# Moving two loads to ScalarE's queue and shortening the store runs of two late chunks in a TensorE-bound pointwise convolution

## Chip, cores, metric

One core of one Trainium2 chip. The metric is device time in microseconds (us); small differences are read from the profile of one execution, since whole runs of one kernel differ by 0.3% and more. Engines: PE = TensorE, DVE = VectorE, ACT = ScalarE, SP = SyncE.

## The reference

A depthwise separable convolution with a 1x1 depthwise kernel: scale each channel by `dw`, then multiply by `pw`.

```python
# x (1,384,384,384), dw (1,1,384), pw (384,384), all bfloat16
out = xp * dw[0, 0]
return jnp.einsum('bhwc,cd->bhwd', out, pw)
```

147,456 rows of 384 channels: 113 MB in, 113 MB out.

## The kernel before

At the start it folds `dw` into `pw` on TensorE (the "weight stage": 18 matmuls, copied to `w_r`). Then 288 "supertiles" of 512 rows pass through: VectorE transposes blocks of x into T, TensorE runs 48 matmuls into one of two PSUM halves, ScalarE copies that half to O, SyncE stores O. x arrives in chunks of 1 to 10 supertiles; SyncE issues all loads and stores but one.

```python
LMAX = 10; NR = 3; LONG = 3
head, tail = [[1, 1, 2, 2, 4]], [[6, 4], [3, 2, 1, 1, 1]]   # supertiles per chunk
...
        def load_x(t):
            ...
            if first + LONG < NS:
                src = rows.rearrange("(p s) c -> p (s c)", p=P)                # long packets
            else:
                src = rows.rearrange("(a k q) c -> q a k c", k=4, q=4)         # 768-byte packets
            if i == 0 and g >= NR:
                nc.sync.wait_ge(s_t[je % 2][1], je // 2 + 1)                   # buffer free
            nc.sync.dma_start(dst, src).then_inc(s_x[g % NR][i], 16)

        def store(t):
            if first + LONG < NS:
                dst = rows.rearrange("(q p j) d -> p q (j d)", q=4, p=P)       # runs of j x 768 bytes
            else:
                dst = rows.rearrange("(m q) d -> m (q d)", q=4)                # 3072-byte runs
            nc.sync.wait_ge(s_a[je % 2], je // 2 + 2)
            if je + 1 == NS:
                nc.sync.wait_ge(s_d, 1)                                        # VectorE's half of the last copy
            nc.sync.dma_start(dst, src).then_inc(s_o[g % NR], 16)

        nc.scalar.dma_start(dw_row[:], ...)
        nc.sync.dma_start(pw_n[:], ...)
        # ... then all loads and stores on SyncE, in the order in which they become possible
```

For a chunk of one supertile either the load or the store is cut into 768-byte packets (the traces hold 1536 loaded packets of that size between 511 and 553 us in the kernel before; the last store shows as 128 packets of 3072 bytes). `LONG = 3` gives the last three chunks long stores and short-packet loads.

## Time and profile before

| | before |
|---|---|
| time, 3 runs | 575.43 us (575.23 to 576.05) |
| span of the profile | 573.7 us |
| main stretch of TensorE starts | 7.18 us |
| 288 supertiles x 1.95 us | 561.6 us |
| last output copies start | 569.0 us |
| last store issued, landed | 570.06, 572.37 us |

Read it as head + TensorE + tail (the head: up to the start of the main stretch; the tail: from the start of the last output copies to the end of the span, 4.7 us here). TensorE never pauses in the main stretch, so only the first 7 and the last 5 us are open to a change in transfers, unless a transfer makes TensorE pause. The profile's lines are with the prediction below.

### The profile page before, as it was taken

Reading aid. Unit: us, or ns where it says so; the run is one execution under the profiler, and the core shown is the slowest. Engines: PE = TensorE matmul, PEld = TensorE weight load, DVE = VectorE, ACT = ScalarE, POOL = GpSimd, SP = SyncE. Lnnn points to the kernel's source line nnn. Section 1 sums busy time; section 2 is a strip of 40 time slices with the busy share of each in tenths; the row PEclk is TensorE's granted clock in tenths of the full one; section 3 lists DMA queues with packets and bytes.
Section 4 is the critical chain, followed back from the end, with each engine's and each line's share of the span. In section 5 each row is a group of like instructions: output and inputs, shape, how many; then the busy total and the mean of one; then the engine's idle time right before and its main releaser. Section 6 shows DMA issues by size and latency. Waiting matters only on the chain.

```text
span 573.7 us, 29706 instructions
## 1 busy us (share of the span) xinstructions
PE 567.3 (99%) x13869; PEld 414.9 (72%) x13869; DVE 509.3 (89%) x583; ACT 418.8 (73%) x296; POOL 0.9 (0%) x8
## 2 busy tenths in 40 slices
PE   8999999999999999999999999999999999999996
PEld 5777777777777777777777777777777777777774
DVE  6899999999999999999999999999999999999994
ACT  6777777777777777777777777777777777777775
POOL 0000000000000000000000000000000000000000
PEclk9999999999999999999999999999999999999999
DMA  8999999999999999999999999999999999994996
GB/s 324 432 409 417 430 397 430 444 424 422 399 408 416 384 397 436 398 383 395 432 398 384 395 429 390 393 401 429 402 385 419 401 390 397 425 394 149 402 408 251
DMA packets 25912, 226.88 MB, mean 395 GB/s; under 512 B 1197, under 2 KB 5678, under 8 KB 22062
## 3 DMA queue, kind: packets, MB, share of 16 engines
q1 hardware_dynamic: 25900, 226.79, 98.0%
q14 instruction: 9, 0.07, 0.0%
q8 instruction: 1, 0.02, 0.0%
q10 hardware_dynamic: 2, 0.00, 0.0%
HBM read 113.54 MB, written 113.25 MB: 395 GB/s over the span
## 4 chain that ended last, share of the span: by engine, by line
PE 98%; DMA 1%; ACT 0%; DVE 0%; issue 0%; SPq 0%
PE ps L166 97%; DMA pw_n<-in_pw_dram 1%; PE ps L216 1%; DMA out_dram<-O 0%; ACT O L307 0%; DVE O L304 0%; SPq L337 0%; SPq L100 0%
## 5 line engine op out<-in xcount | busy, mean ns | idle before, releaser
L166 PE MATMUL ps<-w_r,T 32*128 32x384 bf16 x13824 | 561.8, 321 | 0.1
L258 DVE STREAM_TRANSPOSE T<-X 128x384 uint32<-128x384 uint32 x576 | 506.2, 882 | 54.0 <-DMA X<-in_x_dram 2.4
L307 ACT CAST O<-ps 128x1536 bf16<-128x1536 f32 x288 | 413.5, 1436 | 147.9 <-PE ps L166 147.9
L166 PEld LDWEIGHTS ps<-w_r,T 32*128 32x128 bf16 x13824 | 412.9, 93 | 149.2 <-issue 0.7
L271 ACT CAST w_r<-ps 128x768 bf16<-128x768 f32 x5 | 3.7, 805 | 1.7 <-PE ps L216 1.6
L183 PE MATMUL ps<-zero 32*128 32x384 bf16 x24 | 2.6, 494 | 1.4 <-POOL zero L232 1.4
L304 DVE CAST O<-ps 128x768 bf16<-128x768 f32 x1 | 1.0, 958 | 3.0 <-DMA out_dram<-O 3.0
L216 PE MATMUL ps<-pw_n,sel_w 64*128 64x384 bf16 x18 | 3.0, 510 | 0.1
L183 PEld LDWEIGHTS ps<-zero 32*128 32x128 bf16 x24 | 0.7, 100 | 2.6 <-issue 2.6
L216 PEld LDWEIGHTS ps<-pw_n,sel_w 64*128 64x128 bf16 x18 | 1.2, 138 | 1.6 <-issue 1.2
L244 ACT ACT_TABLE_LOAD x1 | 1.3, 1283 | 1.5 <-SPq L100 1.5
L276 DVE TENSOR_REDUCE sel<-eye 128x64 f32<-128x128 bf16 x1 | 0.3, 290 | 1.8 <-POOL eye L234 1.8
L271 DVE CAST w_r<-ps 128x768 bf16<-128x768 f32 x1 | 1.0, 956 | 1.0 <-PE ps L216 1.0
L286 DVE TENSOR_SCALAR sel_w<-sel,dw_f 128x256 bf16<-128x256 f32 x3 | 0.9, 348 | 0.0
L283 DVE COPY dw_f<-ps 128x3 f32<-128x3 f32 x1 | 0.2, 161 | 0.8 <-PE ps L198 0.8
L198 PEld LDWEIGHTS ps<-ones,dw_row 1*128 1x128 bf16 x3 | 0.2, 98 | 0.2 <-issue 0.2
L244 ACT COPY warm<-warm 128x1 f32<-128x1 f32 x2 | 0.3, 188 | 0.0
L234 POOL TENSOR_SCALAR_AFFINE_SELECT eye<-ones 128x128 bf16<-128x128 bf16 x1 | 0.3, 292 | 0.1
L232 POOL MEMSET zero<- 128x192 uint32 x1 | 0.3, 258 | 0.0
L198 PE MATMUL ps<-ones,dw_row 1*128 1x1 bf16 x3 | 0.2, 159 | 0.0
L233 POOL MEMSET ones<- 128x128 bf16 x1 | 0.2, 204 | 0.0
L231 POOL MEMSET warm<- 128x3 f32 x1 | 0.1, 101 | 0.5 <-SPq L100 0.5
(4 smaller groups left out, 0.4 us busy)
## 6 DMA issues: line engine op xcount, KB each, us to landing
X<-in_x_dram SPq DMA_DIRECT2D x26, 3840.0 KB, 21.5
out_dram<-O SPq DMA_DIRECT2D x26, 3840.0 KB, 27.5
X<-in_x_dram SPq DMA_DIRECT2D x2, 1536.0 KB, 17.4
out_dram<-O SPq DMA_DIRECT2D x2, 1536.0 KB, 13.7
X<-in_x_dram SPq DMA_DIRECT2D x3, 768.0 KB, 8.8
out_dram<-O SPq DMA_DIRECT2D x3, 768.0 KB, 8.9
X<-in_x_dram SPq DMA_DIRECT2D x1, 2304.0 KB, 18.9
out_dram<-O SPq DMA_DIRECT2D x1, 2304.0 KB, 12.1
```

The costliest lines, as they stand in the source:

```text
L166: mm = nc.tensor.matmul(PS[s][:, q, :D], lhsT=Ts[s][32 * q : 32 * q + 32, b, par::2], rhs=w_r[32 * q : 32 * q + 32, b, par, :], start=(b, ...
L183: nc.tensor.matmul(PS[0][:, i, :D], lhsT=zero[32 * i : 32 * i + 32, 0:P], rhs=zero[32 * i : 32 * i + 32, :], start=True, stop=True, tile_p ...
L198: mm = nc.tensor.matmul(PS[1][:, 0, D + k : D + k + 1], lhsT=dw_row[:, P * k : P * k + P], rhs=ones[0:1, 0:1], start=True, stop=True,)
L216: mm = nc.tensor.matmul(PS[(k + 1) % 2][:, 2 * r + v, :D], lhsT=sel_w[64 * v : 64 * v + 64, k, r, :, :].rearrange("p q w -> p (q w)"), rhs ...
L232: nc.gpsimd.memset(zero[:].bitcast(U32), 0).then_inc(s_zero)
L234: nc.gpsimd.affine_select(out=eye[:], in_=ones[:], pattern=[[-1, P]], compare_op=mybir.AluOpType.is_equal, fill=0.0, base=0, channel_multi ...
L244: c = nc.scalar.copy(warm[:, s + 1 : s + 2], warm[:, 0:1])
L258: ins = nc.vector.transpose(out=Tw[:, 3 * h : 3 * h + 3], in_=Xw[:, :, j, 96 * h : 96 * h + 96].rearrange("p k (b w) -> p b k w", w=32),)
L271: o = nc.vector.tensor_copy(out, in_) if e == 0 else nc.scalar.copy(out, in_)
L286: nc.vector.tensor_scalar_mul(sel_w[:, k], sel[:].unsqueeze(2).to_broadcast([P, 2, 4, 32]), dw_f[:, k : k + 1]).then_inc(s_sw)
L304: e = nc.vector.tensor_copy(Ov[:, nq:4, j, :], PS[s][:, nq:4, :D])
L307: a = nc.scalar.copy(Ov[:, 0:nq, j, :], PS[s][:, 0:nq, :D])
```

## The change

Its intent: one load of the slow 768-byte kind (109 GB/s between 528.5 and 530 us in the profile of before, where the transfers around have some 400) in place of three, that one away from SyncE's queue; and the first x chunk issued beside `pw` instead of behind it.

```diff
-LONG = 3
+LONG = 1
-        def load_x(t):
+        def load_x(t, eng=nc.sync):
...
-            if i == 0 and g >= NR:
+            if g >= NR and (i == 0 or eng is not nc.sync):
...
-            nc.sync.dma_start(dst, src).then_inc(s_x[g % NR][i], 16)
+            eng.dma_start(dst, src).then_inc(s_x[g % NR][i], 16)
...
         nc.scalar.dma_start(dw_row[:], ...)
+        load_x(0, nc.scalar)
         nc.sync.dma_start(pw_n[:], ...)
...
-            todo.append((g_end[g - NR] if g >= NR else -1, load_x, t))
+            if 0 < t < NT - LONG:
+                todo.append((g_end[g - NR] if g >= NR else -1, load_x, t))
...
             a.then_inc(s_a[s])
+            if jj == g_end[len(groups) - 1 - NR] + 1:      # supertile 260
+                for u in range(NT - LONG, NT):
+                    load_x(u, nc.scalar)
```

More of the change, by code (lines that the diff above doesn't have):

```diff
@@ L109, in load_x @@
                 src = rows.rearrange("(a k q) c -> q a k c", k=4, q=4)
-            if i == 0 and g >= NR:
+            if g >= NR and (i == 0 or eng is not nc.sync):
                 je = g_end[g - NR]
-                nc.sync.wait_ge(s_t[je % 2][1], je // 2 + 1)
-            nc.sync.dma_start(dst, src).then_inc(s_x[g % NR][i], 16)
+                eng.wait_ge(s_t[je % 2][1], je // 2 + 1)
+            eng.dma_start(dst, src).then_inc(s_x[g % NR][i], 16)
         def store(t):
```

## The prediction

Head +0.45, middle 0, tail +0.05, together +0.5 us on 575.43, so 575.9 us. But the head's +0.45 rests on an assumption, that the packets of the two queues alternate one for one, which no trace had shown when it was made; the counts per engine in it are estimates, packets counted in the trace over the profile's 16 engines. Rival (a)'s 520 to 527 us is an estimate too, from SyncE's three long issues (513.05 to about 530.8 us) and the assumption that ScalarE's would be caught behind them.

> **What bounds the kernel now.** I read the page first (busy shares, then the chain that ended last), then the chain in order of time, then the timeline of the first 10 us, of the stretch around 510 to 530 us, and of the last 5 us, and then the DMA view of short windows. The page and the chain in order of time:
>
> ```profile
> PE 567.3 (99%) x13869; PEld 414.9 (72%) x13869; DVE 509.3 (89%) x583; ACT 418.8 (73%) x296; POOL 0.9 (0%) x8
> PEclk9999999999999999999999999999999999999999
> ...
> 1.01 3.03 DMA pw_n<-in_pw_dram
> 4.05 0.05 issue
> 4.09 2.96 PE ps L216 x18
> 7.05 0.12 issue
> 7.18 557.91 PE ps L166 x13728
> 565.08 0.02 issue
> 565.11 1.45 ACT O L307
> 566.55 0.02 issue
> 566.57 2.46 DMA out_dram<-O
> 569.02 0.94 DVE O L304
> ```
>
> PE is busy 99% at full clock, and the chain is one unbroken PE stretch from 7.18 us on. The starts of ScalarE's output copies confirm it: they stand 1.95 us apart to the end, one per supertile of 48 matmuls, and 288 x 1.95 = 561.6 us is what those matmuls take. (The chain's last two pieces, a store and then the VectorE copy, are an attribution slip: that copy at 569.01 waits for PE's last matmul, as ScalarE's copy at 569.00 does; the semaphore it waits for besides was long satisfied.) So the span of 573.7 us is 7.18 us of head, 561.6 us of PE, and about 4.9 us of tail. A change in transfers can move the time only in three ways: by moving the landing of pw_n (the chain's first piece), by making PE wait in the middle, or by moving the landing of the last store.
>
> The head, from the timeline:
>
> ```profile
> 0.97 0.49 ACTq L131 DMA_DIRECT2D dw_row<-in_dw_dram  x1
> 1.01 0.45 SPq L132 DMA_DIRECT2D pw_n<-in_pw_dram  x1
> 1.49 1.28 ACT L244 ACT_TABLE_LOAD   x1 [1.49 <-SPq L100]
> 1.52 3.49 SPq L113 DMA_DIRECT2D X<-in_x_dram  x7
> 4.09 0.13 PEld L216 LDWEIGHTS ps<-pw_n,sel_w 64*128 64x128 bf16 x4 [0.47 <-DMA pw_n<-in_pw_dram]
> 4.63 3.80 ACT L271 CAST w_r<-ps 128x768 bf16<-128x768 f32 x5 [1.56 <-PE ps L216]
> 5.83 1.55 DVE L258 STREAM_TRANSPOSE T<-X 128x384 uint32<-128x384 uint32 x2
> 8.00 1.57 DVE L258 STREAM_TRANSPOSE T<-X 128x384 uint32<-128x384 uint32 x2 [0.62 <-DMA X<-in_x_dram]
> ```
>
> PE waits for pw_n at 4.09. It does not wait for x: the first transposes (5.83) start without idle time before them, right behind VectorE's weight copy, so the first chunk of x, which landed at 5.0 us, was there in time. VectorE waits 0.62 us for the second chunk, but PE does not notice: the copies from 9.36 us on are already 1.95 us apart. ScalarE has 1.56 us idle before its first weight copy.
>
> The middle, where the three loads of 768-byte packets are issued, in the timeline of SyncE's queue:
>
> ```profile
> 511.42 1.59 SPq L113 DMA_DIRECT2D X<-in_x_dram  x3
> 513.05 8.79 SPq L113 DMA_DIRECT2D X<-in_x_dram  x1
> 521.89 4.44 SPq L113 DMA_DIRECT2D X<-in_x_dram  x1
> 526.38 4.41 SPq L128 DMA_DIRECT2D out_dram<-O  x1
> ```
>
> The reader should see that an issue is normally 0.35 to 0.5 us, but here three in a row hold the queue for 8.79, 4.44 and 4.41 us. In the window 528.5 to 530 us the DMA share is only 0.34 of 16 engines and the rate 109 GB/s, with nearly all packets under 2 KB[...]. It costs nothing: the copies stay 1.95 us apart, since this data is first used near 553 us.
>
> [...]the issues of dw_row (0.97 to 1.46) and pw_n (1.01 to 1.46) overlap almost wholly, neither longer than its neighbours of 0.43 to 0.50 us.[...]
>
> **The change part by part.**
>
> Head: the first x load leaves SyncE's queue, where it was third in line behind pw_n, and goes to ScalarE's, right behind dw_row. Issue time there about 1.5 to 2.0 us, the same as before (1.52).[...] pw_n is 384 packets of 768 bytes, 24 per engine; in the window 2 to 3 us, 229 such packets took 67.5% of 16 engine-us, so 47 ns each, about 1.1 us per engine. The x chunk is 128 packets of 3072 bytes, 8 per engine; in the window of the last store, 570.8 to 572.1 us, 128 such packets took 76.9% of 16 x 1.3 us, so 125 ns each and 1.0 us per engine. pw_n's packets begin about 2.1 us; those of x, half a microsecond later by issue, about 2.6. By 2.6 about a quarter to a third of pw_n has started. If packets alternate one for one, 8 x-packets of 125 ns fall among the remaining 17, and pw_n ends up to 1.0 us later; the engines are only about two thirds busy between 2 and 3 us, so a good half of that falls into time that was idle. I take +0.45 us, with 0 (x still behind[...]) to +0.9 as the bounds. All of it lies on the chain: 18 weight matmuls start at 4.5 instead of 4.09 and the main stretch at 7.6. Nothing is gained in return: x0 was not waited for by PE, and the other chunks going out 0.5 us earlier only shortens VectorE's unfelt waits. ScalarE's second issue pushes its table load to 2.0 and its end to about 3.3, plus 0.3 for two copies = 3.6, still ahead of 4.63.
>
> Middle: [...]SyncE's long blocks vanish. Worth 0, as there is some 40 us of slack. The third is issued by ScalarE after the copy that starts at 516.36 and ends at 517.80:
>
> ```profile
> 516.36 1.44 ACT L307 CAST O<-ps 128x1536 bf16<-128x1536 f32 x1 [0.51 <-PE ps L166]
> 518.30 1.44 ACT L307 CAST O<-ps 128x1536 bf16<-128x1536 f32 x1 [0.51 <-PE ps L166]
> ```
>
> ScalarE idles 0.51 us per supertile, and a copy may be another 0.51 us late (1.95 - 1.44) before PE lacks its PSUM half, so an issue up to about 1.0 us is free. The first such load on SyncE was the third of the group of 1.59 us, so at most about 0.75 us. Expected cost 0. Its wait for transposes of supertile 259 is over: they finished by 511.4, when SyncE's load with the same wait went out.
>
> Tail: the last store is unchanged, 3072-byte runs. The two before it now write 768-byte runs: 32 per engine; in the window 32 to 34 us, 855 packets, nearly all 768-byte, took 102.4% of 32 engine-us, 38 ns each, so 1.2 us against 1.0. The last store is issued at 570.06, its packets run from about 570.9, and the store before it was issued 1.5 us earlier. There is a gap between them of some 0.3 us, so +0.2 us mostly vanishes: I take +0.05.
>
> Sum: +0.45 + 0 + 0.05 = +0.5 us, 575.43 + 0.5 = 575.9 us.
>
> **The rivals.** (a) ScalarE's issue in the middle is caught behind SyncE's blocked one. At 516.4 SyncE now issues the 3840 KB store, with four loads and a previous store (issued 496.37, landed about 525) still queued. [...]ScalarE sits until perhaps 520 to 527 us; less the 1.0 us that is free, PE loses 2 to 8 us: 578 to 584 us. For it: [...]8.79 us of blocking seen on SyncE. Against it: dw_row and pw_n did not delay each other[...]. I give it one in four. (b) [...]pw_n is not disturbed at all: then the head costs 0 and the time is 575.4 to 575.5. (c) Earlier x helps the start: it would need PE to have waited for x; the chain and the 1.95 us spacing say it did not. At most 0.1 us gain. (d) The two 768-byte stores delay the last store by their full 0.2 us each: 576.2.
>
> **Range and chances.** The main case lies between 575.2 and 576.4; rival (a) stretches the upper side. I take 575.1 to 579.5. Faster by 2% would need 11.5 us off a PE stretch that nothing touches: 0.01. Slower by 2% needs a ScalarE stall of over 12 us: 0.03.
>
> **What would show it.** In the chain of the changed kernel, the piece of pw_n should end near 4.5 instead of 4.05 and the L166 stretch begin near 7.6; if it begins at 7.18, the alternation step is wrong. ScalarE's issue near 517.8 should last under 1 us and the copies stay 1.95 us apart; a longer issue and a gap in the PE stretch is rival (a). SyncE's issues at 511 to 513 should all be under 1 us. The last store should land about 3.4 us after PE's end, as now; more would mean the tail step is wrong. The whole is wrong if PE's pace itself changes.

## The result and the profile after

576.14 us median (576.01 to 576.58, 6 runs), against 575.47 us (575.14 to 576.05, 6 runs) for the kernel before in the same rounds. Ratio 1.0011, 95% interval 0.9999 to 1.0024. Ratios here are the mean time of one kernel's fast runs over that of the other's of the same rounds, so not quite the ratio of the medians quoted.

The profile's span grew from 573.70 to 574.27 us, and where it grew is not where the prediction put it. The chain of the changed kernel, in order of time (start, length, what):

```profile
4.49 2.21 ACT w_r L273 x3
6.71 0.14 issue
6.84 561.80 PE ps L168 x13824
...
568.67 0.96 DVE O L306
```

The main stretch starts at 6.84 us, 0.34 earlier, and is as long as before. It no longer waits for the weight matmuls but for ScalarE's three copies of their results. The head, from the timeline:

```profile
1.54 0.37 ACTq L113 DMA_DIRECT2D X<-in_x_dram  x1
3.95 0.13 PEld L218 LDWEIGHTS ps<-pw_n,sel_w 64*128 64x128 bf16 x4 [0.33 <-DMA pw_n<-in_pw_dram]
```

`pw_n` landed at 3.88 us, not later than before (4.05). That gives less than half of the 0.34 us, 0.14 (its first matmul starts at 3.95 instead of 4.09). The rest is the weight stage. Its matmuls' group on the page of before, then of after (busy us, mean ns of one):

```profile
L216 PE MATMUL ps<-pw_n,sel_w 64*128 64x384 bf16 x18 | 3.0, 510 | 0.1
```
```profile
L218 PE MATMUL ps<-pw_n,sel_w 64*128 64x384 bf16 x18 | 2.2, 380 | 0.0
```

Those of them that ran between 5.3 and 6.2 us took 524 ns each before and 325 ns after. In the trace of before, those that start up to 6.31 us took 496 to 524 ns each, and the last two (6.62 us) 424 and 421; in the changed kernel those up to 4.25 us took 496 to 524, two at 4.57 us 451 and 447, and the rest, from 4.86 us on, 319 to 333. The first record of granted clock in the two traces, 1.00, begins at 6.82 and at 4.82 us; before it they hold no record. So the faster pace came 2.0 us earlier in the changed kernel's profile. What sets that moment is not shown. Over all 14 profiles the mean of this group lay between 380 and 521 ns, and it was 502 ns when only the head was changed (`head_only` below): the moved chunk does not fix it, and luck of the run is the natural reading. It is not proved: the nine profiles with the first chunk on ScalarE's queue have 380 to 502 ns (median 414), the five with it on SyncE's 445 to 521 (median 482), and no run tests whether the move shifts the moment.

The middle went as hoped. From the timeline of SyncE's and of ScalarE's queue around 511 us:

```profile
511.08 1.84 SPq L113 DMA_DIRECT2D X<-in_x_dram  x4
516.02 1.44 ACT L309 CAST O<-ps 128x1536 bf16<-128x1536 f32 x1 [0.51 <-PE ps L168]
516.03 0.65 ACTq L113 DMA_DIRECT2D X<-in_x_dram  x1
```

SyncE's long blocks are gone. ScalarE's issue lasts 0.65 us, and it starts with the copy rather than after it: the queue issues while the engine copies, and the next copy starts at 517.97 us, 1.95 us after this one, so it costs nothing at all.

The tail is what grew. The last issue in the timeline of SyncE's queue, the instructions' line in the DMA view of the last 3 us (packets, MB, share of 16 engines), and the store's own line there (KB, us from issue to landing):

```profile
570.08 0.34 SPq L128 DMA_DIRECT2D out_dram<-O  x1
...
q14 instruction: 1, 0.01, 0.6%
...
out_dram<-O SPq DMA_DIRECT2D x1, 384.0 KB, 2.8
```

VectorE's part of the last copy ends at 568.67 + 0.96 = 569.63 us, yet the store goes out at 570.08: 0.45 us of idle queue, where before it was 0.09 (569.97 to 570.06). Then the store takes 2.85 us to land, where it took 2.31. Sum: -0.34 (head) + 0.36 (idle) + 0.54 (landing) = +0.56 us, against 574.27 - 573.70 = 0.57. And in that window one packet of the queue that the profile calls "instruction" (q14, 8192 bytes, at 571.08 us) comes amid the last store's packets. Before, it came at 569.07, ahead of the last store. I call such a packet a fetch, and take it for one of instructions.

### The profile page after: what moved, and what is told of

It is laid out like the page before. It is cut to its first block, busy times and chain, and to the rows that moved or that the text cites. A ratio compares the mean times of both kernels' runs of the same rounds, so it can differ in the third digit from the quotient of the medians.

```text
span 574.3 us, 29706 instructions
## 1 busy us (share of the span) xinstructions
PE 566.5 (99%) x13869; PEld 414.7 (72%) x13869; DVE 507.3 (88%) x583; ACT 419.0 (73%) x296; POOL 0.9 (0%) x8
## 4 chain that ended last, share of the span: by engine, by line
PE 98%; ACT 0%; DVE 0%; issue 0%; POOL 0%; POOLq 0%; SPq 0%
PE ps L168 98%; PE ps L185 0%; ACT w_r L273 0%; DVE O L306 0%; PE ps L218 0%; POOL zero L234 0%; POOL warm L233 0%; PE ps L200 0%; POOLq L343 0%; SPq L100 0%
## 5 line engine op out<-in xcount | busy, mean ns | idle before, releaser
L168 PE MATMUL ps<-w_r,T 32*128 32x384 bf16 x13824 | 561.8, 321 | 0.7 <-ACT w_r L273 0.7
```

Source lines behind the costliest of these rows:

```text
L168: mm = nc.tensor.matmul(PS[s][:, q, :D], lhsT=Ts[s][32 * q : 32 * q + 32, b, par::2], rhs=w_r[32 * q : 32 * q + 32, b, par, :], start=(b, ...
```

## The experiments

The question: is the tail's loss due to the 768-byte stores (theory A1), or to the place of SyncE's instruction fetch, which moves because two issues left SyncE's code (A2)? And does the first chunk's new queue do anything? The runs came in three calls of four kernels each, each call on another chip, each with 5 rounds against the kernel before. All outputs were correct. "SyncE code" counts instructions against before. In the expectation of `head_only`, theory A stands for A1 and A2 together.

| kernel | SyncE code | times, us | ratio [95%] | main start | copy start to last issue | issue to landing | last fetch at |
|---|---|---|---|---|---|---|---|
| before | 0 | 575.23 to 576.05 | | 7.18 | 1.06 | 2.31 | 569.07 |
| changed | -2 | 576.01 to 576.58 | 1.0011 [0.9999, 1.0024] | 6.84 | 1.41 | 2.85 | 571.08 |
| `head_only` | -1 | 575.35 to 577.17 | 1.0000 [0.9984, 1.0016] | 7.09 | 1.07 | 2.88 | 570.87 |
| `long1_sync` | 0 | 575.35 to 576.52 | 0.9996 [0.9982, 1.0010] | 7.07 | 1.05 | 2.32 | 569.79 |
| `after_x0_sync` | -1 | 575.57 to 576.22 | 0.9996 [0.9981, 1.0011] | 7.23 | 1.06 | 2.58 | 570.85 |
| `after_again` | -2 | 575.69 to 576.22 | 1.0000 [0.9985, 1.0015] | 6.84 | 1.41 | 2.54 | 570.74 |
| `after_pad2` | -2+2 | 575.22 to 575.74 | 0.9999 [0.9986, 1.0012] | 6.98 | 1.06 | 2.31 | 569.10 |
| `after_pad8` | -2+8 | 575.07 to 576.15 | 0.9994 [0.9981, 1.0007] | 7.06 | 1.05 | 3.16 | 535 |
| `long3_rest` | -2 | 575.70 to 579.24 | 1.0025 [1.0007, 1.0043] | 6.99 | 1.44 | 3.99 | 572.31 |
| `before_again` | 0 | 575.27 to 577.88 | 1.0015 [0.9997, 1.0033] | 7.04 | 1.05 | 2.31 | 568.77 |
| `pad8_again` | -2+8 | 575.09 to 575.50 | 0.9997 [0.9983, 1.0010] | 7.17 | 1.06 | 2.32 | 535 |
| `pad8_long3` | -2+8 | 575.26 to 575.85 | 1.0001 [0.9987, 1.0014] | 6.95 | 1.06 | 2.83 | 539 |
| `pad8_long0` | -1+8 | 575.73 to 576.47 | 1.0011 [0.9997, 1.0025] | 7.07 | 1.06 | 3.44 | 554 |
| `pad8_x0_sync` | -1+8 | 575.27 to 575.65 | 1.0000 [0.9986, 1.0014] | 7.08 | 1.06 | 2.41 | 554 |

The right-hand columns are of the one profiled execution of each kernel. With eight added instructions the last fetch in the table is another one: the changed kernel has a fetch at 534.8 us too, and the one that moved lies at 520.3 us in `after_pad8` and 520.4 in `pad8_again`. `before_again`: the same program against itself came out at 1.0015. Of the changes only the 1.0025 of `long3_rest` has an interval that excludes 1, and only just. So the reasons rest on the profiles and on where runs of several kernels fall, not on a ratio.

### Taking the change apart

**head_only**: before, with the first x chunk on ScalarE's queue.

```diff
         nc.scalar.dma_start(dw_row[:], ...)
+        load_x(0, nc.scalar)
```

> Only the first chunk of x moves to ScalarE's queue, behind the tiny dw row; all else as before. Theory A (the two short stores and the third load at the end cost the added 0.6 us; the head's gain of 0.34 us in the one profile is luck[...], since the weight matmuls' mean fell from 510 to 380 ns there while pw_n landed only 0.17 us earlier): time equal to before within 0.2 us, tail from last matmul to end of span 4.7 us as before; the head 6.8 or 7.2 us depending on the weight matmuls' mean. Theory B[...]: pw_n lands after 4.3 us and the time is +0.3 us or more. Theory C (the head move truly gains): -0.3 us against before.

Measured: median 575.95 us. `pw_n` landed at 3.96 us: the delay that my prediction expected (theory B) does not exist. The main stretch began at 7.09 us with weight matmuls of 502 ns: the 0.34 us gain of the first profile (theory C) does not follow from this move. But the tail was 5.3 us, not 4.7, with all three last stores in the old 3072-byte form: the store landed 2.88 us after its issue and the fetch fell at 570.87. Theory A1 cannot explain that.

**long1_sync**: before, with only the constant changed.

```diff
-LONG = 3
+LONG = 1
```

> Only the constant goes from 3 to 1, all loads stay on SyncE's queue: the stores of the last chunk but one and but two write 768-byte runs. Theory A1 (the short runs of the store before the last cost the tail): tail from last matmul to the span's end about 5.6 us as in the changed kernel, against 4.7 before; time +0.7 us with the same head. Theory A2 (the tail's loss comes from where an instruction fetch falls, 571.08 us in the changed kernel's profile, amid the last store, 569.07 before): the fetch moves since SyncE's or ScalarE's code differs, and the tail follows it, 4.7 to 5.6 us, whatever the run length.

Measured: median 575.80 us. Tail 4.70 us, landing 2.32 us, fetch at 569.79: short runs in the stores before the last cost nothing, as A2 says. This profile shows something else. Its chain, in order of time:

```profile
7.07 19.76 PE ps L166 x480
26.83 0.41 issue
27.24 542.31 PE ps L166 x13344
```

TensorE paused after exactly 10 supertiles (480 matmuls). VectorE's timeline around it, of this kernel and then of the kernel before:

```profile
26.28 4.36 DVE L258 STREAM_TRANSPOSE T<-X 128x384 uint32<-128x384 uint32 x6 [2.42 <-DMA X<-in_x_dram]
```
```profile
25.26 5.45 DVE L258 STREAM_TRANSPOSE T<-X 128x384 uint32<-128x384 uint32 x7 [1.37 <-DMA X<-in_x_dram]
```

The sixth chunk of x landed at 26.18 us here and at 25.16 before, where TensorE did not notice. The main stretch lasts 562.5 us here against 561.8, so the late chunk cost 0.7 us. An estimate from these figures: a landing 0.7 us earlier (25.5 us, or 25.6 with the start at 7.18) would have cost nothing, so the kernel before stands about 0.4 us from a pause that my reading (the waits for x are "unfelt") took for safe.

**after_x0_sync**: the changed kernel, first chunk back on SyncE.

```diff
-        load_x(0, nc.scalar)
-            if 0 < t < NT - LONG:
+            if t < NT - LONG:
```

> The changed kernel, but the first chunk of x stays on SyncE's queue. Theory A1 (short runs): tail about 5.6 us, time +0.7 us against before if the head is 7.18 us, +0.3 us if it is 6.84. If the head's move were a true gain of 0.34 us (theory C), this must be 0.3 us slower than the changed kernel in the same rounds. If the tail goes back to 4.7 us, neither the runs nor the third load are to blame, but the place of SyncE's code.

Measured: median 575.73 us. One instruction fewer on SyncE than before: no idle time ahead of the last store (1.06), but the fetch at 570.85 and landing 2.58 us. Theory C expected this kernel to be 0.3 us slower than the changed one; the medians are 575.73 and, for `after_again` in the same rounds, 575.99. But its tail was 0.3 us shorter (5.0 against 5.3), which would hide a gain of 0.3 us at the head, and the main start was 7.23 against 6.84: this pair does not settle C. The pair without a late fetch (`pad8_again`, `pad8_x0_sync`) starts at 7.17 and 7.08, against C.

**after_again**: the changed kernel unaltered.

> The changed kernel once more, to see what of its first profile repeats: the time 0.5 to 0.8 us above before; the tail of 5.6 us and the idle 0.41 us of SyncE ahead of the last store, if they are of the kernel; the head at 6.84 us again only if it is not luck[...].

Measured: median 575.99 us, 0.44 above before's median of these rounds (575.55), though the means are equal, since before's 11 runs reach from 575.14 to 577.14. The idle 0.45 us ahead of the last store repeats to the hundredth, and again a fetch falls amid that store. The early main start (6.84) came back too, with weight matmuls of 414 ns; later profiles of the same head start at 6.95 to 7.17. This time the chain before the main stretch is another one, in order of time:

```profile
1.54 4.31 DMA X<-in_x_dram
...
5.87 0.87 DVE T L260
...
6.84 561.81 PE ps L168 x13824
```

TensorE waits here for the first chunk of x itself. On ScalarE's queue that chunk landed at 5.29 to 6.09 us in nine profiles, on SyncE's at 4.88 to 5.06 in five: the load that was to come sooner comes later. In four of the nine (`after_again`, `after_pad2`, `long3_rest`, `pad8_long0`) the main stretch hangs on it, in none of the five.

### Moving SyncE's code and nothing else

**after_pad2** and **after_pad8**: the changed kernel, with two or eight instructions on SyncE that do nothing but raise an unused semaphore, after its first store.

```diff
+            if f is store and t == 0:
+                for _ in range(2):                         # 8 in after_pad8
+                    nc.sync.nop(nofuse=True).then_inc(s_pad)
```

> The changed kernel with two do-nothing instructions (increments of an unused semaphore) on SyncE after its first store, so that SyncE has as many instructions as in the kernel before. Theory A2 (SyncE's own instruction fetch falls into the last store because two issues left its code): the last 8192-byte fetch moves ahead of the last store (before 570.1 us), the idle time of SyncE ahead of the last store falls from 0.45 to about 0.1 us, the last store lands 2.3 us after its issue instead of 2.5 to 2.9, and the tail is 4.7 us instead of 5.3 to 5.6. Theory A1 (the 768-byte stores): nothing changes, tail 5.3 us or more.

Measured: 575.34 us median. Two do-nothing instructions give back the whole tail: idle 0.10 us, landing 2.31 us, tail 4.70 us, fetch at 569.10. The DMA view of the same final window (570.45 to 573 us, the share of the DMA engines in tenths in 40 slices) of the changed kernel, with its instruction queue's line, and then of this one, which has no such line:

```profile
DMA  0000000779797999999899720101010000000000
...
q14 instruction: 1, 0.01, 0.8%
```
```profile
DMA  4101999989797979797400000000000000000000
```

In the changed kernel the last store's packets start three slices (some 0.2 us) later, as it was issued 0.22 us later (570.08 against 569.86), and after the bulk of them a thin trail (the digits 2 0 1 0 1 0 1) runs on: its packets of 3072 bytes start at 571.98, 572.10, 572.22 and 572.33 us, one after the other, 121 ns each. Here it ends at once, and the instruction packet is not in the window.

> As the former, with eight. Theory A2: the fetch moves earlier still (some ten us before the end), tail 4.7 us, and with the fuller start of x the time is the lowest of all, 575.1 to 575.4 us in nearly every run, 0.6 us under the changed kernel. Theory A1: tail 5.3 us or more, time as the changed kernel.

Measured: median 575.08 us, four of five runs at 575.07 to 575.63, and the profiled one 576.15. In that profile the fetch had moved to 54 us from the end (a fetch at 520.3 us is new, and none comes after that at 535), the idle time was gone, and still the store landed 3.16 us after its issue. The DMA rate in 40 slices, 569 to 573 us, of this profile and of its repeat `pad8_again`:

```profile
GB/s 31 15 31 192 338 338 323 338 323 338 323 323 338 323 315 177 31 115 330 422 392 422 392 330 422 422 392 300 31 31 31 31 31 0 31 31 31 0 0 0
```
```profile
GB/s 23 23 23 23 146 323 346 307 353 323 315 353 315 323 353 315 200 39 31 369 399 399 492 307 399 430 369 461 246 31 0 0 0 0 0 0 0 0 0 0
```

The trail of 31 GB/s is one packet of 3072 bytes per 0.1 us slice, where such a packet takes some 0.12 us (124 ns on average in the last store of the kernel before). My estimate from these two figures is that one engine still works when the others are done; the traces do not name the engine of a packet. Without the trail, in the repeat, the store landed 0.84 us sooner after its issue (2.32). So a late landing has two candidates: the fetch (in all five profiles where one falls amid the last store, the landing took 2.54 us or more; in the four where it came just ahead of the issue, 2.31 or 2.32), and an engine that lags by chance of the run (theory D). The fetch's packet took 0.31 us in the changed kernel, less than the 0.54 us that its landing grew, so the fetch alone need not be all of it.

**long3_rest**: the changed kernel's two moved loads, with the old constant's stores and loads.

```diff
-LONG = 1
+LONG = 3        # the last load alone on ScalarE
```

> The change without its constant: the first chunk of x and the last load go on ScalarE's queue, but the last three chunks keep 3072-byte stores (and 768-byte loads). Theory A2: the tail is that of the changed kernel, 5.3 to 5.6 us, with 0.45 us of idle SyncE ahead of the last store, since SyncE has the same number of instructions; time as the changed kernel. Theory A1: tail 4.7 us, 0.6 to 0.9 us faster than the changed kernel.

Measured: median 576.88 us (575.70 to 579.24), on the same chip and in the same rounds as the padded kernels' 575.34 and 575.08. The idle time is there again (0.48 us), with three long stores: it belongs to the number of SyncE's instructions, not to the runs. The last store landed only 3.99 us after its issue, with a fetch at 572.31 and a trail of 42 to 113 GB/s up to some 572.8 us. Theory A2 gets its idle time here, but not its number for the tail: 6.8 us, not 5.3 to 5.6, and the ratio of 1.0025 is worse than the changed kernel's two (1.0011, 1.0000; other chips).

**before_again**: no edit.

> The kernel before, once more, for a second profile of it. If the sixth chunk of x (the second group of ten) is on a knife's edge, landing 25 to 26 us and wanted by 25.8, then of its runs some are near 575.2 and others 0.7 us or more above, and the profile shows either a landing under 25.8 us and no gap in TensorE's stretch, or a later one and a gap; the tail is 4.7 us in either case. The main stretch starts at 6.8 to 7.2 us with the mean of the weight matmuls between 380 and 520 ns.

Measured: 575.27 to 577.88 us; four runs at 575.27 to 575.68, two at 577.85 and above. The profile fell on a fast one: sixth chunk at 24.81 us, no pause, tail 4.69 us. What the two long runs did is not in a profile.

### The parts, with the fetch out of the way

**pad8_again**: as `after_pad8`.

> The changed kernel with eight do-nothing SyncE instructions, again: in its first trial four of five runs were at 575.07 to 575.63 and the profiled one at 576.15, where one or two DMA engines were still busy with an earlier store when the last one came (landing 3.16 us after issue with no fetch near). Theory A2 plus D (D: an engine that lags at the end, by chance of the run, delays the last store): most runs 575.0 to 575.4, none above 576.6, no fetch after 560 us; tail 4.7 us or, where an engine lags, more. If instead A2 is wrong, its times are those of the changed kernel, 575.7 to 576.6.

Measured: 575.09 to 575.50, tail 4.70 us. Of all fifteen runs of the padded changed kernel, fourteen lie at 575.74 or below; of the eleven runs of the changed kernel, two do (575.69, 575.73). The chips differ, so this is no ratio; the kernel before had medians of 575.47 and 575.55 beside the changed kernel and of 575.44 and 575.34 beside the padded one.

**pad8_long3**: as `long3_rest`, with the eight instructions.

> The same with the last three chunks in the old form: 3072-byte stores, and three loads of 768-byte packets[...], two of them on SyncE. Theory D: [...]an engine that lags is likelier; then the times have a long upper tail (one or more of six above 576.6), a median 0.3 us or more above its sibling with the constant 1, and the last store lands more than 2.5 us after its issue in the profile if that run is a long one. If the constant does not matter, its times are those of its sibling.

Measured: 575.26 to 575.85, median 0.2 us above its sibling, none above 576.6. The upper tail that theory D expected is absent, in this kernel and in the kernel before of these rounds (575.19 to 575.88). A late landing shows in the profile (2.83 us without a fetch near), but that the three 768-byte loads make it likelier is not shown.

**pad8_long0**: no chunk in the old form, so the last store too in 768-byte runs. The last load then goes back to SyncE's queue, as the loop for ScalarE's late load is empty.

```diff
-LONG = 1
+LONG = 0
```

> The same with no chunk in the old form: [...]the last store too writes 768-byte runs, 32 packets of about 38 ns per engine instead of 8 of 125, so its landing should take 2.5 us instead of 2.3 us from its issue: +0.2 us against its sibling with 1. Theory D: no run above 576.6 us. If the run length mattered more than its packets[...], landing over 3 us.

Measured: median 576.42 us; 575.73 twice, 576.42 to 576.47 three times. The median is 1.2 us above its sibling's, and the runs do not overlap (575.09 to 575.50 there). In the profiled run the last store landed 3.44 us after its issue, where the sibling took 2.32. That is more than the packet count gives (+0.2 us, the estimate above), and the rate again trails off at the end, at 23 to 27 GB/s; with five runs the two cannot be separated. In this kernel the last store should stay in long runs.

**pad8_x0_sync**: first chunk on SyncE.

```diff
-        load_x(0, nc.scalar)
-            if 0 < t < NT - LONG:
+            if t < NT - LONG:
```

> The same as the changed kernel with eight do-nothing instructions, but the first chunk of x on SyncE's queue. Theory E (the second queue fills the DMA engines early, so that the sixth chunk of x lands near 23.9 us instead of 24.6 to 26.2): 4 to 6 us moves 250 to 320 GB/s instead of 390 to 425, the sixth chunk lands 24.6 us or later, and one or two of six runs are 0.5 us or more above the rest where TensorE waits for it near 26.5 us; the fastest runs equal those of its sibling. If the queue does not matter, the rates and landings equal the sibling's.

Measured: 575.27 to 575.65, median 0.2 us above its sibling. The outlier that theory E expected is absent; the transfers behaved as it says. Busy time of the engines in two stretches of the head, the last two columns being DMA share and GB/s, for the kernel before and then the changed one:

```profile
4.00:6.00 2.00, 1.93 (x18) 0.92 (x16) 1.04 (x2) 1.37 (x2) 0.00 (x0) 1.00 0.90 253
6.00:8.00 2.00, 1.88 (x29) 0.93 (x29) 1.38 (x3) 1.90 (x4) 0.00 (x0) 1.00 0.86 335
```
```profile
4.00:6.00 2.00, 2.00 (x22) 0.82 (x18) 1.19 (x2) 1.51 (x3) 0.00 (x0) 1.00 1.05 421
6.00:8.00 2.00, 1.32 (x32) 0.88 (x34) 2.00 (x4) 2.00 (x3) 0.00 (x0) 1.00 1.02 427
```

Without exception in 14 profiles: with the first chunk on SyncE (five) 250 to 321 GB/s between 4 and 6 us and the sixth chunk landed at 24.6 to 26.2 us; with it on ScalarE (nine) 389 to 424 GB/s and 23.7 to 24.1 us. That takes the kernel away from the pause of `long1_sync`, 0.7 us that one of the five profiles had. The pauses were too rare in these rounds to show in a median. Why the rate is lower with one queue, no run tells. Idle engines are not the whole of it: `before_again` moved 250 GB/s at a DMA share of 1.06. And the move has two parts that no run separates, the second queue and the other loads' issues, which all go out about half a microsecond earlier (the second chunk's at 1.51 us, before at 2.03).

## Why the prediction was right or wrong

The time (576.14 us) lies in the range and near the 575.9 predicted, and no change of 2% came, as it said. The account of where the time would go was wrong at both ends. The loss itself is not established by the times: the ratios of the changed kernel are 1.0011 [0.9999, 1.0024] and 1.0000 [0.9985, 1.0015].

- **What bounds the kernel**: right. 561.8 us of the main stretch in every profile without a pause; only head and tail moved.
- **Head, +0.45 us**: wrong. The step that failed is the start of x's packets, "about 2.6", and with it "`pw_n` ends up to 1.0 us later". In the nine profiles with the chunk on ScalarE, `pw_n` landed at 3.87 to 4.10 us; in the five with it on SyncE, at 3.91 to 4.09. The queues of the changed kernel from 2 to 3 us, then from 3 to 4 us, show why:

```profile
q1 hardware_dynamic: 217, 0.17, 72.5%
...
q10 hardware_dynamic: 76, 0.23, 59.0%
q1 hardware_dynamic: 193, 0.16, 49.5%
```

  ScalarE's queue (q10) moves no packet between 2 and 3 us, though the chunk was issued at 1.54 to 1.91; over the nine profiles its first packet starts at 2.97 to 3.22. By 3.0 us 217 of the 384 packets of `pw_n` have started. The assumed alternation agrees with the trace: from 3.93 to 4.4 us, when `pw_n` is in, the two queues moved 32 and 31 packets. For `pw_n` it is the outcome of rival (b), "pw_n is not disturbed". What holds the chunk back is not shown. (The first load of x was second in SyncE's queue, not "third in line"; nothing rests on it.)
- **"Nothing is gained in return"**: wrong in part, and it missed a loss. The second to sixth chunks land earlier, the sixth by about a microsecond, and the wait that this shortens is unfelt by a margin of only about 0.4 us. But the first chunk lands 0.2 to 1.2 us later, while packets of the second one move beside its own (the 32 and 31 above), and in four of nine profiles TensorE's start hangs on it (`after_again` above). The prediction's "x0 was not waited for by PE" held for the kernel before alone.
- **Middle, 0**: right, and safer than argued. Rival (a), a blocked ScalarE, did not occur: 0.65 us, beside a copy. (How many engines these loads use is not shown: a share of 0.34 of 16 is over five, and a share is no count of engines, since it reached 1.11 between 3 and 4 us. What the trace shows is a rate of 109 GB/s where the transfers around it have some 400.)
- **Tail, +0.05 us**: wrong in size and cause. The profile shows +0.36 us idle ahead of the last store and +0.54 us in its landing. Rival (d), the 768-byte stores, is refuted by `long1_sync`. Nothing in the prediction asked what taking two instructions from SyncE does. `after_pad2` shows that the idle time (0.45 us, then 0.10) and the place of the fetch (571.08 us, then 569.10) follow the count of SyncE's instructions; that the added 0.36 us of idle time is SyncE waiting for its own instructions is the natural reading, but argued. The late fetch itself cannot be what the store's issue waited for: it starts at 571.08 us, a microsecond after the issue.

So the nearness of the number is luck. In the first profile the head was -0.34 us where +0.45 was said, and the tail +0.90 where +0.05 was said (+0.59 in `after_again`): two misses of 0.5 to 0.9 us that nearly cancelled. That profile alone would have supported a third story, "the head gained 0.34 us", which the repeats do not bear out: the main stretch starts at 6.84 to 7.17 us with the chunk on ScalarE (nine profiles, median 6.99) and at 7.04 to 7.23 on SyncE (five, median 7.08).

What stays open: what makes SyncE idle; what the long runs of unchanged kernels (up to 577.88 us) do; how much of a late landing is the fetch and how much a lagging engine, where both occur; whether the constant 1 lowers the risk of a lag.

No version beats the kernel before beyond noise. The changed kernel with its instruction count restored is the best candidate: medians 575.34, 575.08 and 575.26 us, ratios 0.9999, 0.9994 and 0.9997.

## What to carry to other kernels

Where one engine is busy 99%, look for what can still move in the head and tail alone, and treat a wait ahead of that engine as safe only after computing its margin. Repeat the profile before believing a change of a third of a microsecond: the moment at which the weight matmuls go from 524 to some 325 ns, and a trail of late packets, are of that size (the first profile's 0.34 us at the head and 0.54 in the landing). When a change adds or removes instructions on a queue that ends the kernel, look for the instruction packets in the DMA view, and pad the queue to tell their place from the change itself.
